# Attention inside a fused block: scores in a ring of four single PSUM banks, two of four exponentials in halves, and another order of TensorE's steps

## The chip, the cores and the metric

The kernel runs on one core of a Trainium2 chip. The metric is the device time of one execution in microseconds. A second figure is the span, from the first to the last instruction in the profile of one execution. In the text PE (or TensorE) is the matrix engine, PEld its weight load, DVE VectorE, ACT ScalarE, POOL GpSimd, and SP the engine that issues most DMAs. PSUM is the memory that TensorE writes, in eight banks; one bank holds 512 fp32 columns of 128 rows.

## The reference

One transformer block on x of 2048 x 512: pre-norm attention with 32 heads of width 16, then a gated MLP with a spatial mixing matrix.

```python
def _A_ref(x, wqkv, wo):
    B, S, D = x.shape
    H = 32; Dh = D // H
    qkv = (x @ wqkv).reshape(B, S, 3, H, Dh).transpose(2, 0, 3, 1, 4)
    q, k, v = qkv[0], qkv[1], qkv[2]
    scale = Dh ** -0.5
    scores = jnp.einsum("bhqd,bhkd->bhqk", q, k) * scale
    p = _softmax(scores, axis=-1)
    o = jnp.einsum("bhqk,bhkd->bhqd", p, v)
    return o.transpose(0, 2, 1, 3).reshape(B, S, D) @ wo
...
x = A_x
h = x + _A_ref(_layernorm(x, axis=-1), A_wqkv, A_wo)
h2 = h + _B_ref(_layernorm(h, axis=-1), B_w_in, B_w_sp, B_b_sp, B_w_out)
```

Only the attention is touched by the change. The gated MLP, `_B_ref`, is computed after it.

## The kernel before

**Stages.** First the projections to q, k and v (until about 162 us), then the attention loop (until about 1333 us), then the MLP. While the loop runs, GpSimd prepares the MLP's matrices from a list of chores that is handed out by the turn of the loop.

**Units of the attention.** Four heads form a group (`hg`, 8 of them), 512 queries a block (`qb`, 4), 128 keys a block (`kb`, 16). A unit is (hg, qb, kb); there are 512. One turn of the loop does two units, kb and kb1 = kb + 1, so there are 256 turns. The order in which each engine gets its instructions is the order in which the loop writes them (`manual_schedule`, L541); no scheduler moves them.

**Scores and exponentials.** `score` (L776) makes, for one pair p of two of the four heads, two matmuls (t = 0 and 1) of 128 keys by 512 queries, each into one bank of a tile `s` of two banks; t = 0 uses rows 0 to 49 of the matrix engine's array, t = 1 rows 64 to 113, so that two such matmuls can run side by side. One ScalarE instruction (L787) takes the exponential of all 128 x 1024 into an SBUF tile `pt`. The tiles `s` come from a pool of two (`ps_s`, L772). A unit has two such pairs, a turn four.

**Weighing.** `weigh` (L790) multiplies the values with the four exponentials of a unit, four fp32 matmuls side by side in columns of the array, and adds up over the 16 key blocks in the bank `pv`. In a turn it is called for the second unit of the turn before and for the first unit of this one. After the last key block `gather` (L798) copies `pv` out.

**Maxima.** The softmax needs each query's maximum before its scores are exponentiated. For a later block `max_pair` (L204) computes the scores of 128 queries a second time, the other way round (queries in the rows), in eight steps a turn, each a matmul of 48 rows into one of three banks `m0` to `m2`: four steps for t = 1 (`one(1, e)`) and two for t = 0 (`one(0, 2)`, `one(0, 3)`, here named `last`), each read by a VectorE maximum (L227); and for the remaining two quarters of t = 0 sums and differences of keys: `minus`, whose bank ScalarE reads with an Abs into `ab` (L232), and `plus`, whose bank VectorE reads together with `ab` (L236). Every eighth turn the maxima of 1024 rows are collected (L242 to L248) and turned by `max_rows` (L254), a VectorE transpose and eight DMAs.

The bank of each step is given by hand, as the argument of `step`: 2, 0, 1, 2, 0, 1, 2, 1. Eleven of the 256 sets of maxima (`LEAD`) are made ahead of the loop, between the projections (`ahead`, L531). So the last 11 turns have no maxima; their three banks then go to a pool `later`, and every third score tile is taken from there.

**A turn's order on TensorE** (L1043 to L1066): scores (kb, 0) and (kb, 1), two steps, `weigh` of the unit before, two steps (`minus` and `one(1, 1)`), scores (kb1, 0), a step, scores (kb1, 1), two steps (`one(1, 3)`, `plus`), `weigh` of kb, the step `last`. ScalarE's order: two exponentials, Abs, two exponentials.

Of the kernel before, what the change touches and what calls it, by code (L numbers as in the profile page):

```python
# [8 lines left out]
F32 = mybir.dt.float32  # L9
# [18 lines left out]
NB = S // P  # L28
HB = NB // 2
NQ = S // 512  # L30
# [4 lines left out]
KM = 50  # L35
PB = 6
FIRST = 2
RG = 64
# [20 lines left out]
def block_kernel(ctx: ExitStack, tc: tile.TileContext, x, wqkv, wo, w_in, w_sp4, b_sp, w_out, out):  # L59
# [7 lines left out]
    nc = tc.nc  # L67
# [131 lines left out]
    def bank(i):  # L199
        if i in more:  # L200
            return more[i]()
        return ps_m.tile([P, 512], F32, name=f"m{i}")

    def max_pair(m):  # L204

        g, i = divmod(m, 8)  # L210
        hg, qb = divmod(g, NQ)
        q, k, w = qst[g], kst[hg % 2], uvs[hg % 2]
        if i == 0:
            mx[g] = sm.tile([P, 16, 4], F32, name="mx")
            nc.gpsimd.memset(mx[g][:, :8, 3:], LOW)
        c, p = slice(i % 4 * P, i % 4 * P + P), i // 4
        at = lambda t, e: mx[g][:, t * 8 + i, e:e + 1]

        def scores(t, keys, b):
            r = slice(RG * t, RG * t + KS)  # L220
            acc = bank(b)
            nc.tensor.matmul(acc, q[r, p, c], keys[r, p], start=True, stop=True)  # L222
            return acc

        def one(t, e, b):
            acc = scores(t, k[:, :, 512 * e:512 * e + 512], b)
            nc.vector.reduce_max(at(t, e if t else e - 1), acc, axis=AX.X)  # L227

        def minus(b):
            acc = scores(0, w[:, :, 512:], b)  # L230
            ab[0] = sm.tile([P, 512], F32, name="ab")
            nc.scalar.activation(ab[0], acc, AF.Abs)  # L232

        def plus(b):
            acc = scores(0, w[:, :, :512], b)
            nc.vector.tensor_tensor_reduce(ab[0], acc, ab[0], 0.5, LOW, ALU.add, ALU.max, at(0, 0))  # L236

        def last(b):
            one(0, 3, b)
            if i == 7:  # L240
                nm = sm.tile([P, 2, 8], F32, name="nm")
                nc.vector.tensor_reduce(nm.rearrange("p t i -> p (t i)"), mx.pop(g), axis=AX.X,  # L242
                                        op=ALU.max, negate=True)
                parts = sm.tile([P, 2, 2, 8], F16, name="mparts")
                nc.gpsimd.tensor_scalar(nm, nm, 1.0 / ONE, 1.0, op0=ALU.mult, op1=ALU.mult)  # L245
                nc.gpsimd.tensor_copy(parts[:, :, 0], nm)
                nc.gpsimd.tensor_sub(parts[:, :, 1], nm, parts[:, :, 0])
                turned[0] = (g, parts)  # L248

        ab = {}  # L250
        four = [lambda b, e=e: one(1, e, b) for e in range(4)]
        return [four[0], lambda b: one(0, 2, b), minus, four[1], four[2], four[3], plus, last]

    def max_rows():  # L254

# [12 lines left out]
    with ExitStack() as pre:  # L268
        p2 = pre.enter_context(tc.tile_pool(name="pre_2", bufs=2))
        pc = pre.enter_context(tc.tile_pool(name="pre_c", bufs=1))  # L270
        pt = pre.enter_context(tc.tile_pool(name="pre_pt", bufs=2, space=PSUM))
# [257 lines left out]
        todo, done = [], [0]  # L529

        def ahead(k):  # L531
            for _ in range(k):
                m = done[0] // 8
                if not todo and m < LEAD:
                    steps = max_pair(m)
                    todo.extend(steps[i] for i in (0, 1, 3, 2, 4, 6, 5, 7))
                if todo:
                    todo.pop(0)(done[0] % 5)
                    done[0] += 1
# [67 lines left out]
        for g in range(3):  # L607
            a, b = 4 * g, 4 * g + 4
# [54 lines left out]
        for j in range(24):  # L663
            b, n, i = 1 + j // 8, j // 2 % 4, 1 - j % 2
# [21 lines left out]
            if j == 20:  # L686
                scales_ = [nc.scalar.alloc_register(f"scale{b}") for b in range(DB)]
# [78 lines left out]
    with ExitStack() as at:  # L766
# [2 lines left out]
        uvs.append(kpool1.tile([KS, 2, 1024], F16, name="uvs1"))  # L769
        fixed(kst[1])  # L770
        pp = at.enter_context(tc.tile_pool(name="pp", bufs=6))
        ps_s = at.enter_context(tc.tile_pool(name="ps_s", bufs=2, space=PSUM))  # L772
        ps_v = at.enter_context(tc.tile_pool(name="ps_v", bufs=1, space=PSUM))
        pv = {}

        def score(hg, qb, kb, p):  # L776

            q, k = qst[hg * NQ + qb], kst[hg % 2]
            turn[0] += len(later)
            pool = later[0] if turn[0] % 3 == 2 else ps_s  # L780
            s = pool.tile([P, 2, 512], F32, name="s")
            for t in range(2):
                r = slice(RG * t, RG * t + KM)
                nc.tensor.matmul(s[:, t, :], k[r, p, kb * P:(kb + 1) * P], q[r, p, :],  # L784
                                 start=True, stop=True)
            t = pp.tile([P, 2, 512], F32, name="pt")
            nc.scalar.activation(t, s, AF.Exp, scale=scales_[hg // 2])  # L787
            return t

        def weigh(hg, qb, kb, pts):  # L790
            if kb == 0:
                pv[0] = ps_v.tile([P, 512], F32, name="pv")
            for j in range(4):
                c = (4 * kb + j) * VW
                nc.tensor.matmul(pv[0][32 * j:32 * j + 32, :], vst[hg % 2][:, c:c + 32],  # L795
                                 pts[j % 2][:, j // 2, :], start=kb == 0, stop=kb == NB - 1)

        def gather(hg, qb, pool=sm):  # L798

# [39 lines left out]
        pool = nc.gpsimd  # L839
# [179 lines left out]
        prev, turn, later, asked = None, [0], [], []  # L1019
        for n in range(0, len(units), 2):  # L1020
            (hg, qb, kb), (_, _, kb1) = units[n:n + 2]
            if m % 8 < 7 and n < 480:
                work(4.1 if m % 8 < 6 else 2.0)
            if n == 480:
                work(None)
            if hg + 1 < HG and n % 64 < 24 and n % 4 == 0:
                load_k(hg + 1, [n % 64 // 4])
            if hg + 1 < HG and n % 64 < 12 and n % 4 == 2:
                load_uv(hg + 1, [n % 64 // 4])
            if hg + 1 < HG and n % 64 == 30:  # L1030
                copy_v = load_v(hg + 1)
# [10 lines left out]
            step = lambda b: steps and steps.pop(0)(b)  # L1042
            pts = [score(hg, qb, kb, 0), score(hg, qb, kb, 1)]  # L1043
            step(2)
            step(0)
            if prev is None:

                pv[0] = ps_v.tile([P, 512], F32, name="pv")
                for j in range(4):
                    nc.tensor.matmul(pv[0][32 * j:32 * j + 32, :], vst[0][:, :32],  # L1050
                                     vst[0][:, :512], start=True, stop=True)
            else:
                weigh(*prev)
            step(1)
            if kb == 0 and n:
                gather(*units[n - 1][:2])
            step(2)
            pts1 = [score(hg, qb, kb1, 0)]
            step(0)
            pts1.append(score(hg, qb, kb1, 1))  # L1060
            step(1)
            step(2)
            weigh(hg, qb, kb, pts)
            if turned:
                max_rows()
            step(1)  # L1066
            prev = (hg, qb, kb1, pts1)
            if kb == 6 and n > NB:
                invert()
            if n in (486, 490, 506):  # L1070
                asked.append(load_o(h_rows[min((n - 486) // 4, 2)]))
            if n in (492, 496, 508):
                asked.pop(0)()
            if n in (494, 502):
                split_o(h_rows[(n - 494) // 8])
            if n in (500, 504):
                sb = h_rows[(n - 500) // 4]
                make_h(sb, later[0].tile([P, 512], F32, name="h"))
# [26 lines left out]
    with ExitStack() as mid:  # L1105
# [3 lines left out]
        pt = mid.enter_context(tc.tile_pool(name="mid_pt", bufs=2, space=PSUM))  # L1109
# [278 lines left out]
```

## Time and profile before

| | |
|---|---|
| Median of three runs | 1776.86 us (1776.65 to 1778.52) |
| The profiled execution | 1777.92 us |
| Its span | 1775.8 us |
| Granted clock of TensorE, mean | 0.999 |
| First exponential, last maximum in the loop, start of the MLP | 162.1, 1284.8, 1333.4 us |

How to read the profile's lines. A group's line names the source line, the engine, the operation, the tile written, the tile read, the shapes and the count; behind the first bar stand the busy time in us and the mean of one instruction in ns, behind the second the idle time of the engine just before these instructions and what ended most of it. A line of the timeline has the start in us, the time from the first start to the last end of a merged run of equal instructions, and in brackets the idle time before it with its releaser. A line of a window has its bounds, its length, the busy time and count of PE, PEld, DVE, ACT and POOL, then the granted clock, the share of the DMA engines and GB/s. Ends of matmuls are modelled. Two instructions of one engine can overlap in the record, because the next begins before the last has written its end; the distance of two starts is the pace.

### The profile page before, as it was taken

How to read it: one execution, taken by the hardware profiler on the slowest of the kernel's cores; microseconds unless marked ns; L12 is line 12 of the kernel's file. 1: busy time of each engine (PE TensorE's matmuls, PEld its weight loads, DVE VectorE, ACT ScalarE, POOL GpSimd, SP SyncE). 2: the span in 40 equal slices, each digit the busy share in tenths (PEclk: the TensorE clock that was granted, in tenths of full speed). 3: DMA queues.
4: the chain of work that ended last, by engine and by line, in shares of the span. 5: the costliest groups of instructions: out<-in, count | busy, mean ns of one | idle time of the engine just before them, and what ended most of it. 6: DMA issues, size and time to landing. Idle time of an engine off the chain costs nothing.

```text
span 1775.8 us, 33083 instructions
## 1 busy us (share of the span) xinstructions
PE 1735.6 (98%) x11621; PEld 659.6 (37%) x11621; DVE 1409.4 (79%) x2896; ACT 1270.4 (72%) x1614; POOL 826.1 (47%) x1088
## 2 busy tenths in 40 slices
PE   9999999999999999999999999999998999999999
PEld 4433222222222222222222222222225666777776
DVE  7688999999999999999999999999926876111112
ACT  4335999999999999999999999999984555001000
POOL 1322677765762167776677757700003766010010
PEclk9999999999999999999999999999999999999999
DMA  5534332342220134435345434300033563753450
GB/s 178 158 102 147 79 83 83 79 90 69 70 66 21 56 115 126 139 115 138 92 115 135 132 100 130 98 19 9 13 71 109 139 176 112 269 196 129 148 187 24
DMA packets 183806, 191.47 MB, mean 108 GB/s; under 512 B 66344, under 2 KB 135016, under 8 KB 183640
## 3 DMA queue, kind: packets, MB, share of 16 engines
q1 hardware_dynamic: 181336, 183.72, 35.5%
q10 hardware_dynamic: 2304, 5.64, 0.8%
q8 instruction: 91, 1.49, 0.4%
q14 instruction: 75, 0.61, 0.1%
HBM read 124.40 MB, written 64.29 MB: 106 GB/s over the span
## 4 chain that ended last, share of the span: by engine, by line
PE 61%; ACT 17%; issue 9%; DVE 6%; DMA 2%; POOL 2%; SPq 1%; ACTq 0%; DVEq 0%; POOLq 0%
PE pv L795 17%; PE m L222 13%; ACT pt L787 11%; PE s L784 6%; ACT ab L232 5%; PE acc L106 4%; PE acc L108 4%; PE acc L107 4%; PE g L106 4%; PE g L108 4%; PE g L107 4%; DVE mx L227 1%; DMA rc<-r_scr 1%; DVE rs_t L123 1%; DVE rs_u L125 1%
## 5 line engine op out<-in xcount | busy, mean ns | idle before, releaser
L787 ACT ACTIVATE pt<-s 128x1024 f32<-128x1024 f32 x1024 | 995.8, 1037 | 75.4 <-PE s L784 71.8
L227 DVE TENSOR_REDUCE mx<-m 128x1 f32<-128x512 f32 x1511 | 963.7, 684 | 27.8 <-PE m L222 10.4
L795 PE MATMUL pv<-pt,vst 128*32 128x512 f32 x4096 | 551.9, 605 | 0.8 <-ACT og L802 0.8
L222 PE MATMUL m<-kst,qst 48*128 48x512 f16 x1511 | 479.3, 379 | 18.8
L784 PE MATMUL s<-qst,kst 50*128 50x512 f16 x2048 | 420.4, 379 | 2.3 <-DVE mx L227 0.6
L222 PEld LDWEIGHTS <-qst 48*128 48x128 f16 x2048 | 147.1, 94 | 539.5 <-issue 504.7
L784 PEld LDWEIGHTS <-kst 50*128 50x128 f16 x2048 | 141.5, 94 | 152.9 <-issue 75.3
L245 POOL TENSOR_SCALAR nm<-nm 128x16 f32<-128x16 f32 x32 | 6.6, 206 | 399.3 <-DVE nm L242 378.2
L222 PE MATMUL m<-uvs,qst 48*128 48x512 f16 x503 | 191.8, 381 | 0.0
L236 DVE CUSTOM_DVE_ANT_0 ab<-m,ab 128x512 f32<-128x512 f32 x252 | 171.7, 681 | 0.4 <-PE m L222 0.4
L232 ACT ACTIVATE ab<-m 128x512 f32<-128x512 f32 x251 | 151.1, 602 | 18.9 <-PE m L222 18.8
L795 PEld LDWEIGHTS pv<-pt,vst 128*32 128x32 f32 x4096 | 82.9, 108 | 183.3 <-issue 167.2
L1257 ACT ACTIVATE pT<-tp 128x384 fp32r<-128x384 f32 x32 | 14.0, 488 | 142.0 <-PE tp L1249 142.0
L1335 POOL TENSOR_TENSOR pr<-pr,z 128x344 f32<-128x344 f32 x8 | 7.3, 912 | 193.4 <-DVE pr L1334 193.4
L964 POOL TENSOR_TENSOR op<-raw,op 128x512 f16<-128x512 f32 x80 | 92.7, 1159 | 5.8
L871 POOL TENSOR_TENSOR raw<-raw 128x512 f32<-128x512 f32 (+1 forms) x84 | 83.3, 991 | 6.3
L876 POOL TENSOR_TENSOR acc_sp<-acc_sp,raw 128x512 f32<-128x512 f32 x63 | 80.3, 1275 | 4.5
L1279 DVE TENSOR_TENSOR y<-acc,h 128x512 f32<-128x512 f32 x16 | 11.1, 692 | 85.8 <-PE acc L1275 84.4
L106 PE MATMUL acc<-wi,hT 128*128 128x344 f16 x256 | 79.1, 309 | 0.0
L107 PE MATMUL acc<-wi,hT 128*128 128x344 f16 x256 | 79.1, 309 | 0.0
L108 PE MATMUL acc<-wi,hT 128*128 128x344 f16 x256 | 79.1, 309 | 0.0
L724 POOL TENSOR_TENSOR o<-o,rc 128x512 f32<-128x512 f32 x16 | 20.3, 1270 | 99.1 <-DMA rc<-r_scr 74.5
(233 smaller groups left out, 2300.4 us busy)
## 6 DMA issues: line engine op xcount, KB each, us to landing
raw<-in_w_sp SPq DMA_DIRECT2D x128, 256.0 KB
s_scr<-op SPq DMA_DIRECT2D x64, 256.0 KB
op<-s_scr SPq DMA_DIRECT2D x32, 512.0 KB
a_scr<-op SPq DMA_DIRECT2D x48, 256.0 KB
op<-a_scr SPq DMA_DIRECT2D x24, 512.0 KB
qst<-q_scr SPq DMA_DIRECT2D x192, 32.0 KB
kst<-k_scr SPq DMA_DIRECT2D x48, 128.0 KB
raw<-in_w_in SPq DMA_DIRECT2D x32, 172.0 KB
```

The costliest lines, as they stand in the source:

```text
L106: nc.tensor.matmul(ps, lh, rh, start=first, stop=False, **kw)
L107: nc.tensor.matmul(ps, lh, rl, start=False, stop=False, **kw)
L108: nc.tensor.matmul(ps, ll, rh, start=False, stop=last, **kw)
L222: nc.tensor.matmul(acc, q[r, p, c], keys[r, p], start=True, stop=True)
L227: nc.vector.reduce_max(at(t, e if t else e - 1), acc, axis=AX.X)
L232: nc.scalar.activation(ab[0], acc, AF.Abs)
L236: nc.vector.tensor_tensor_reduce(ab[0], acc, ab[0], 0.5, LOW, ALU.add, ALU.max, at(0, 0))
L784: nc.tensor.matmul(s[:, t, :], k[r, p, kb * P:(kb + 1) * P], q[r, p, :], start=True, stop=True)
L787: nc.scalar.activation(t, s, AF.Exp, scale=scales_[hg // 2])
L795: nc.tensor.matmul(pv[0][32 * j:32 * j + 32, :], vst[hg % 2][:, c:c + 32], pts[j % 2][:, j // 2, :], start=kb == 0, stop=kb == NB - 1)
L871: pool.tensor_mul(got[0] if n else acc, got[0], got[0])
L964: chores.append((lambda: pool.tensor_sub(t[0][:, 1], of(), t[0][:, 0]), TT))
```

## The change

- The four score banks become one tile `s4` of four banks, taken once ahead of the loop from a pool of one. `score` makes one matmul (one t) into one bank; a turn of two banks is chosen by a counter. In the last 11 turns a third tile `s2` from `later` joins.
- `exps` takes the exponential of two banks or, for the first pair of kb and the second pair of kb1 in turns that have maxima, of one bank at a time: two instructions of 128 x 512 in place of one of 128 x 1024.
- TensorE's order in a turn is new: step, three scores, two steps, the fourth score, `weigh` of the unit before, two steps, two scores, a step, two scores, two steps, `weigh` of kb.
- The steps' order is new (`minus` becomes the fifth, `plus` the last, `last` goes into the list `two`), and their banks go round: the count of steps modulo three. Ahead of the loop the order is changed accordingly.

```diff
-        def last(b):
-            one(0, 3, b)
             if i == 7:
...
         four = [lambda b, e=e: one(1, e, b) for e in range(4)]
-        return [four[0], lambda b: one(0, 2, b), minus, four[1], four[2], four[3], plus, last]
+        two = [lambda b, e=e: one(0, e, b) for e in (2, 3)]
+        return [four[0], four[1], two[0], four[2], minus, two[1], four[3], plus]
...
-                    todo.extend(steps[i] for i in (0, 1, 3, 2, 4, 6, 5, 7))
+                    todo.extend(steps[i] for i in (0, 2, 1, 5, 3, 4, 6, 7))
...
-        ps_s = at.enter_context(tc.tile_pool(name="ps_s", bufs=2, space=PSUM))
+        ps_s = at.enter_context(tc.tile_pool(name="ps_s", bufs=1, space=PSUM))
         ps_v = at.enter_context(tc.tile_pool(name="ps_v", bufs=1, space=PSUM))
+        s4 = ps_s.tile([P, 4, 512], F32, name="s")
...
-        def score(hg, qb, kb, p):
...
-            s = pool.tile([P, 2, 512], F32, name="s")
-            for t in range(2):
-                r = slice(RG * t, RG * t + KM)
-                nc.tensor.matmul(s[:, t, :], k[r, p, kb * P:(kb + 1) * P], q[r, p, :],
-                                 start=True, stop=True)
-            t = pp.tile([P, 2, 512], F32, name="pt")
-            nc.scalar.activation(t, s, AF.Exp, scale=scales_[hg // 2])
-            return t
+        def score(hg, qb, kb, p, t):
+
+            if not t:
+                turn[0] += 1
+                where = turn[0] % (2 + len(later))
+                s = later[0].tile([P, 2, 512], F32, name="s2") if where == 2 else s4[:, 2 * where:2 * where + 2]
+                pts[p, kb] = (s, pp.tile([P, 2, 512], F32, name="pt"))
+            r = slice(RG * t, RG * t + KM)
+            nc.tensor.matmul(pts[p, kb][0][:, t, :], kst[hg % 2][r, p, kb * P:(kb + 1) * P],
+                             qst[hg * NQ + qb][r, p, :], start=True, stop=True)
+
+        def exps(hg, kb, p, t=slice(0, 2)):
+            s, w = pts[p, kb]
+            nc.scalar.activation(w[:, t, :], s[:, t, :], AF.Exp, scale=scales_[hg // 2])
...
-            pts = [score(hg, qb, kb, 0), score(hg, qb, kb, 1)]
-            step(2)
-            step(0)
+            def step():
+                if steps:
+                    steps.pop(0)(count[0] % 3)
+                    count[0] += 1
+
+            halves = bool(steps)
+
+            def both(k, p, t):
+                score(hg, qb, k, p, t)
+                if halves and (k, p) in ((kb, 0), (kb1, 1)):
+                    exps(hg, k, p, t)
+                elif t:
+                    exps(hg, k, p)
+
+            step()
+            both(kb, 0, 0)
+            both(kb, 0, 1)
+            both(kb, 1, 0)
+            step()
+            step()
+            both(kb, 1, 1)
...
                 weigh(*prev)
-            step(1)
             if kb == 0 and n:
                 gather(*units[n - 1][:2])
-            step(2)
-            pts1 = [score(hg, qb, kb1, 0)]
-            step(0)
-            pts1.append(score(hg, qb, kb1, 1))
-            step(1)
-            step(2)
-            weigh(hg, qb, kb, pts)
+            step()
+            step()
+            both(kb1, 0, 0)
+            both(kb1, 0, 1)
+            step()
             if turned:
                 max_rows()
-            step(1)
-            prev = (hg, qb, kb1, pts1)
+            both(kb1, 1, 0)
+            both(kb1, 1, 1)
+            step()
+            step()
+            weigh(hg, qb, kb)
+            prev = (hg, qb, kb1)
```

More of the change, by code (lines that the diff above doesn't have):

```diff
@@ L771, in block_kernel, with weigh @@
         pp = at.enter_context(tc.tile_pool(name="pp", bufs=6))
-        ps_s = at.enter_context(tc.tile_pool(name="ps_s", bufs=2, space=PSUM))
+        ps_s = at.enter_context(tc.tile_pool(name="ps_s", bufs=1, space=PSUM))
         ps_v = at.enter_context(tc.tile_pool(name="ps_v", bufs=1, space=PSUM))
+        s4 = ps_s.tile([P, 4, 512], F32, name="s")
         pv = {}
-        def score(hg, qb, kb, p):
-            q, k = qst[hg * NQ + qb], kst[hg % 2]
-            turn[0] += len(later)
-            pool = later[0] if turn[0] % 3 == 2 else ps_s
-            s = pool.tile([P, 2, 512], F32, name="s")
-            for t in range(2):
-                r = slice(RG * t, RG * t + KM)
-                nc.tensor.matmul(s[:, t, :], k[r, p, kb * P:(kb + 1) * P], q[r, p, :],
-                                 start=True, stop=True)
-            t = pp.tile([P, 2, 512], F32, name="pt")
-            nc.scalar.activation(t, s, AF.Exp, scale=scales_[hg // 2])
-            return t
-        def weigh(hg, qb, kb, pts):
+        def score(hg, qb, kb, p, t):
[10 more added lines that the diff above has]
+            nc.scalar.activation(w[:, t, :], s[:, t, :], AF.Exp, scale=scales_[hg // 2])
+        def weigh(hg, qb, kb):
             if kb == 0:
@@ L795, in weigh @@
                 nc.tensor.matmul(pv[0][32 * j:32 * j + 32, :], vst[hg % 2][:, c:c + 32],
-                                 pts[j % 2][:, j // 2, :], start=kb == 0, stop=kb == NB - 1)
+                                 pts[j % 2, kb][1][:, j // 2, :], start=kb == 0, stop=kb == NB - 1)
+            for p in range(2):
+                del pts[p, kb]
         def gather(hg, qb, pool=sm):
@@ L1018, in block_kernel @@
         units = [(hg, qb, kb) for hg in range(HG) for qb in range(NQ) for kb in range(NB)]
-        prev, turn, later, asked = None, [0], [], []
+        prev, turn, count, later, asked, pts = None, [1], [0], [], [], {}
         for n in range(0, len(units), 2):
@@ L1041, in block_kernel @@
                     tc.tile_pool(name="ps_l", bufs=1, space=PSUM, side="right")))
-            step = lambda b: steps and steps.pop(0)(b)
-            pts = [score(hg, qb, kb, 0), score(hg, qb, kb, 1)]
-            step(2)
-            step(0)
+            def step():
[16 more added lines that the diff above has]
+            both(kb, 1, 1)
             if prev is None:
```

## The prediction

> **What bounds the kernel now.** I read the page first (busy shares, chain, groups), then the stages as windows, then the chain and the timeline of one turn of the attention loop. Page:
>
> ```profile
> PE 1735.6 (98%) x11621; PEld 659.6 (37%) x11621; DVE 1409.4 (79%) x2896; ACT 1270.4 (72%) x1614; POOL 826.1 (47%) x1088
> ...
> L787 ACT ACTIVATE pt<-s 128x1024 f32<-128x1024 f32 x1024 | 995.8, 1037 | 75.4 <-PE s L784 71.8
> L227 DVE TENSOR_REDUCE mx<-m 128x1 f32<-128x512 f32 x1511 | 963.7, 684 | 27.8 <-PE m L222 10.4
> L795 PE MATMUL pv<-pt,vst 128*32 128x512 f32 x4096 | 551.9, 605 | 0.8 <-ACT og L802 0.8
> L222 PE MATMUL m<-kst,qst 48*128 48x512 f16 x1511 | 479.3, 379 | 18.8
> L784 PE MATMUL s<-qst,kst 50*128 50x512 f16 x2048 | 420.4, 379 | 2.3 <-DVE mx L227 0.6
> L784 PEld LDWEIGHTS <-kst 50*128 50x128 f16 x2048 | 141.5, 94 | 152.9 <-issue 75.3
> L236 DVE CUSTOM_DVE_ANT_0 ab<-m,ab 128x512 f32<-128x512 f32 x252 | 171.7, 681 | 0.4 <-PE m L222 0.4
> L232 ACT ACTIVATE ab<-m 128x512 f32<-128x512 f32 x251 | 151.1, 602 | 18.9 <-PE m L222 18.8
> ```
>
> Three engines are nearly full, and the share alone doesn't say which sets the pace. The stages, as windows:
>
> ```profile
> 162.10:1284.80 1122.70, 1101.65 (x7840) 288.55 (x7837) 1098.19 (x2093) 1054.11 (x1255) 656.18 (x860) 1.00 0.32 88
> 1284.80:1333.40 48.60, 46.98 (x296) 10.88 (x294) 10.96 (x31) 42.23 (x47) 4.45 (x6) 1.00 0.33 76
> 1333.40:1776.00 442.60, 428.98 (x2715) 290.35 (x2712) 176.73 (x502) 113.83 (x208) 126.66 (x159) 1.00 0.45 149
> ```
>
> The first window (span, then PE, PEld, DVE, ACT and POOL busy, clock, DMA) is the attention loop while it also makes maxima: 256 - 11 = 245 turns in 1122.7 us, **4.58 us a turn**. Then 11 turns without maxima (48.6 us), then all that the change does not touch. One turn in the chain of waits:
>
> ```profile
> 742.09 0.50 ACT ab L232
> 742.63 0.43 PE m L222 x2
> 743.06 1.00 PE pv L795 x8
> 744.06 0.32 PE m L222
> ...
> 744.91 0.72 issue
> 745.63 1.02 ACT pt L787
> 746.64 0.50 ACT ab L232
> ```
>
> From one Abs to the next (742.09 to 746.64, 4.55 us): Abs frees a maxima bank, TensorE, which goes strictly in order, gets past the step that waited for that bank, does a `weigh` (1.00), and only then the scores for which ScalarE stands idle. So a turn is a loop of waits between TensorE and ScalarE, not a full engine. Price of each hop (timeline of one turn):
>
> ```profile
> 734.85 0.68 PE L784 MATMUL s<-qst,kst 50*128 50x512 f16 x3
> 735.14 0.09 PEld L784 LDWEIGHTS <-kst 50*128 50x128 f16 x1 [0.19 <-issue]
> 735.36 0.40 PE L222 MATMUL m<-kst,qst 48*128 48x512 f16 x2
> 735.64 1.02 ACT L787 ACTIVATE pt<-s 128x1024 f32<-128x1024 f32 x1 [0.54 <-PE s L784]
> 735.68 0.63 PE L795 MATMUL pv<-pt,vst 128*32 128x512 f32 x3
> ```
> ```profile
> 733.13 1.96 ACT L787 ACTIVATE pt<-s 128x1024 f32<-128x1024 f32 x2
> 735.64 1.94 ACT L787 ACTIVATE pt<-s 128x1024 f32<-128x1024 f32 x2 [0.54 <-PE s L784]
> 737.46 0.60 ACT L232 ACTIVATE ab<-m 128x512 f32<-128x512 f32 x1
> 737.94 1.04 ACT L787 ACTIVATE pt<-s 128x1024 f32<-128x1024 f32 x1
> ```
> ```profile
> 736.68 0.39 PE L222 MATMUL m<-uvs,qst 48*128 48x512 f16 x1
> ...
> 738.12 0.37 PE L222 MATMUL m<-kst,qst 48*128 48x512 f16 x1
> ```
> ```profile
> 147.64 0.38 PE L222 MATMUL m<-uvs,qst 48*128 48x512 f16 x1
> ...
> 148.09 0.60 ACT L232 ACTIVATE ab<-m 128x512 f32<-128x512 f32 x1 [2.36 <-PE m L222]
> ```
>
> - An exponential ends at 733.13 + 1.96 = 735.09, and the score that waited for its bank starts with its weights at 735.14: **0.05** from ScalarE to TensorE. The same at 738.12, behind the Abs that ended at 738.06.
> - A lone matmul started at 147.64 is read at 148.09: **0.45** from TensorE to ScalarE. For a pair of scores (735.15) it is **0.49** (735.64).
> - A matmul on rows just used starts **0.21** after the one ahead of it (735.15 to 735.36).
> - `weigh` starts 0.32 after the last small matmul (735.36 to 735.68) and lets the next one through 1.00 later (736.68): **1.32**.
> - Abs to exponential: **0.48** (737.46 to 737.94).
>
> **The change part by part.** *What it says*: a score no longer waits for a two-bank tile but for one bank, and the first and fourth exponential of a turn become halves, so that each starts behind one matmul. *What the changed program does* is told by its list of instructions with the counts they wait for. All four banks are one tile, `s4`, taken once ahead of the loop. Of a steady turn (h: a half, F: a whole exponential; kb, kb1 the two key blocks; the newest ScalarE instruction that must have ended is on the right):
>
> ```
> S(kb,0,0)    waits for h(kb1,1,1) of the turn before
> S(kb,0,1)    waits for h(kb,0,0)     (other bank)
> S(kb,1,0)    waits for h(kb,0,1)     (other bank)
> S(kb,1,1)    no further wait
> S(kb1,0,0)   waits for F(kb,1)       (other bank)
> S(kb1,0,1)   no further wait
> S(kb1,1,0)   waits for F(kb1,0)      (other bank)
> S(kb1,1,1)   waits for h(kb1,1,0)    (other bank)
> ```
>
> Each score waits for the last exponential that read **any** of the four banks. Before, each waited for the exponential two tiles back. So the ring is a ring of one: score, exponential, score, exponential. That is the whole forecast; everything else is small beside it.
>
> One turn, with TensorE's new order (M0 to M7 the steps; M4 is `minus`, whose reader is Abs): M0, S, S, S, M1, M2, S, weigh, M3, M4, S, S, M5, S, S, M6, M7, weigh. A half is taken at the 0.60 of the Abs of the same 128x512 (L232); bounds: above half of a 1024 (0.52), below a whole one (1.04). From the turn's first score at 0:
>
> 1. h(kb,0,0): 0.45 + 0.60 + 0.05 = 1.10, S(kb,0,1) starts.
> 2. h(kb,0,1): 1.10 more, S(kb,1,0) at 2.20.
> 3. M2 uses the same rows: +0.21; S(kb,1,1) beside it, at 2.41.
> 4. `weigh` of the unit before: +1.32, M3 and M4 at 3.73. F(kb,1) runs meanwhile (2.41 + 0.45 to 3.90) and is covered.
> 5. M4 to Abs +0.49 (a pair), Abs to F(kb1,0) +0.48: 4.70. The scores for it start at 3.95 and would be ready at 4.44, so Abs, queued ahead of it on ScalarE, decides.
> 6. F(kb1,0) 1.04 + 0.05: S(kb1,1,0) at 5.79.
> 7. h(kb1,1,0): +1.10, S(kb1,1,1) at 6.89.
> 8. M6, M7 behind it +0.21, `weigh` +1.32: 8.42, the next turn's M0 and S. Its own wait, for h(kb1,1,1), ended at 6.89 + 1.10 = 7.99 and is covered.
>
> Sum: 3 x 1.10 + 2 x 0.21 + 2 x 1.32 + 0.49 + 0.48 + 1.09 = **8.42 us** against 4.58: +3.84 x 245 = **+940 us**.
>
> *Costs at nothing.* Two more ScalarE instructions a turn (4 x 0.60 for 2 x 1.04, +0.33 us of recorded time) lie in ScalarE's new idle time, apart from the halves counted above. VectorE has 6 x 0.68 + 0.68 = 4.8 us of work in 8.4, so the rotation of the maxima's banks frees each long before its M. GpSimd's queue is handed out by turns, not by time, and has more room; SP's few DMAs a turn likewise, and the maxima's transpose with its eight DMAs, which stands some instructions earlier, has a whole group of turns until its rows are read. The order of steps ahead of the loop changes for 11 maxima under projections: nothing, within 3 us.
>
> *The 11 turns without maxima.* No halves; a third tile joins the rotation, but two of three uses are still in `s4`. By the same hops six exponentials (three units, with three `weigh`) take about 7.25 us, so a turn of four 4.83 against 48.6/11 = 4.42: +5 us.
>
> *The clock.* TensorE will have gaps of some 1.2 us (from M5 at 4.2 to S(kb1,1,0) at 5.8) and be busy about 60% of a turn. Rows that bear on it:
>
> ```profile
> 1333.40:1336.80 3.40, 1.25 (x9) 0.51 (x6) 2.26 (x3) 1.48 (x3) 1.27 (x1) 1.00 0.20 59
> ```
> ```profile
> 1369.25 0.61 PE L106 MATMUL acc<-wo,o 128*128 128x512 f16 x1 [2.58 <-ACT o L729]
> 1369.65 0.63 PE L107 MATMUL acc<-wo,o 128*128 128x512 f16 x1
> ```
>
> In a window with 1.25 of 3.40 us busy the clock stayed 1.00; only behind 2.58 us of nothing does a matmul take 0.61 and the next start 0.40 later. So I count the full clock. The Trainium skill, "TensorE: Matmul & The Clock Gate" (section "A second HAM failure mode: psum-queue depth-cycling"), speaks against it: a kernel that cycles through PSUM banks can idle briefly so often that the clock swings between half and full. No stretch of this trace shows that; it is a rival below.
>
> **Forecast.** The profiled execution took 1777.92 us, 2.1 more than its span; 1775.8 + 940 + 5 + 2.1 = 2723. It stood 1.1 above the median, so **2722 us**.
>
> **Rivals.**
>
> - *The waits are per bank after all* (the change does what it says). Then VectorE's maxima decide:
>
> ```profile
> 699.37 3.07 DVE L227 TENSOR_REDUCE mx<-m 128x1 f32<-128x512 f32 x5
> ...
> 702.36 0.68 DVE L236 CUSTOM_DVE_ANT_0 ab<-m,ab 128x512 f32<-128x512 f32 x1
> ```
>
>   Reductions start (3.07 - 0.68)/4 = 0.60 apart. Three of them (1.80), `plus` and its release (0.74), M2 to S 0.21, `weigh` 1.32, M3 to its reduction 0.45: 4.52 for a turn, at most 0.21 less if that score pairs with M2; with the 0.03 by which the mean now exceeds the chain, 4.55 or 4.34: 1777 - 7 = 1770, at best 1777 - 59 = 1718. Faster, if the wait counts don't mean what I read. 3%.
> - *`weigh` and Abs leave the loop*: scores and exponentials alone, 4 x 1.10 + 2 x (0.49 + 1.09) = 7.56: 1777 + 245 x 2.98 + 5 = 2512. It needs TensorE to run a `weigh` while a score ahead of it waits; in the chain above it never does. Up to 2640 for mixtures. 8%.
> - *Dearer hops*: weights loaded only behind each wait (94 ns by the page, five times a turn) and 0.49 at each of three halves: 8.42 + 0.47 + 0.12 = 9.01, 2867. The 0.05 measured at a waiting score speaks against it. 6%.
> - *Half clock*: 0.21 becomes 0.40, `weigh` doubles its 1.00, each of four hops to ScalarE takes 0.23 more (0.61 for 0.38): 8.42 + 0.38 + 2.00 + 0.92 = 11.7, about 3530; part of the time, near 3100. 5%.
>
> **How the numbers follow.** The forecast has 78%, for turns of 8.2 to 8.75 us: 2670 to 2805. The range takes in the near ends of the second and third rival: 2640 to 2850. A measurement here can tell some 0.2% from no change. The first rival splits into faster 2% and the same 1%; slower 97%.
>
> **What would show it.** Right: 980 exponentials of 128x512 near 0.60 and 534 of 128x1024; the stage with maxima near 2063 us, a turn 8.4; ScalarE and VectorE each near 60% busy there; ScalarE idle for scores and TensorE for exponentials, in turn; clock 1.00; the last stage still 443 us. Wrong: two scores of different banks running ahead of one exponential (waits per bank), a `weigh` of more than 1.0 us (clock), or a score that starts well over 0.05 behind the exponential that it waits for.

## The result and the profile after

| | before | changed |
|---|---|---|
| Median | 1777.53 us (4 runs) | 3400.99 us (4 runs, 3387.42 to 3410.3) |
| Ratio of the medians | | 1.9128, 95% interval 1.9089 to 1.9166 |
| Profiled execution, span | 1777.92, 1775.8 us | 3387.42, 3385.4 us |
| Mean granted clock of TensorE | 0.999 | 0.663 |
| Mean distance of two Abs (one turn) | 4.58 us | 11.11 us |

The change nearly doubles the time. The forecast was 2722 us with a range up to 2850: the direction was right, the size was far off.

The page of the changed kernel, with the lines that answer to those shown of before (busy time and share of each engine; the clock in forty slices, in tenths; the groups):

```profile
PE 2628.2 (78%) x11621; PEld 701.8 (21%) x11621; DVE 1477.6 (44%) x2896; ACT 1432.4 (42%) x2104; POOL 821.5 (24%) x1088
...
PEclk9955565555555565566556566555655566999999
...
L788 ACT ACTIVATE pt<-s 128x512 f32<-128x512 f32 (+1 forms) x1514 | 1128.6, 747 | 1199.8 <-PE s L783 1062.4
L783 PE MATMUL s<-qst,kst 50*128 50x512 f16 x2048 | 935.5, 558 | 740.6 <-ACT pt L788 740.6
L795 PE MATMUL pv<-pt,vst 128*32 128x512 f32 x4096 | 897.5, 964 | 0.0
L222 PE MATMUL m<-kst,qst 48*128 48x512 f16 x1510 | 810.9, 577 | 0.0
```

Two things are to be seen, and they are different. First, the idle times at the right ends: ScalarE was idle 71.8 us for scores before, now 1062.4; TensorE's scores waited 2.3 us, now 740.6, all of it for exponentials. The two engines work in turn. Second, the same matmuls take longer: a score 558 ns on the mean for 379, a `weigh` matmul 964 for 605. The counts of matmuls are equal (11621). The clock line fits this: about half speed from the third slice to the end of the attention loop.

The stages, as windows (span, PE, PEld, DVE, ACT, POOL, clock, DMA share, GB/s): the turns with maxima, those without, and the rest:

```profile
162.10:2892.00 2729.90, 2001.02 (x7890) 332.39 (x7889) 1165.86 (x2094) 1223.02 (x1754) 654.44 (x864) 0.58 0.13 37
2892.00:2950.00 58.00, 44.95 (x278) 12.33 (x277) 13.70 (x34) 37.54 (x42) 3.81 (x3) 0.94 0.20 50
2950.00:3386.00 436.00, 423.62 (x2682) 287.18 (x2680) 174.04 (x497) 111.78 (x204) 124.57 (x158) 0.99 0.45 150
```

The whole loss lies in the first window, where the clock is 0.58. From the first exponential to the last Abs of the loop there were 1120.3 us before (162.1 to 1282.4) and 2714.2 now (161.7 to 2875.9): +1594. From there to the end of the span 493.4 became 509.5: +16. Together that is the 1610 us by which the spans differ.

The list of waits in the first window (who waits for whom: us in all, times, longest) shows the ring:

```profile
ACT pt L788 <- PE s L783: 1049.7, 985, 2.3
PE s L783 <- ACT pt L788: 729.4, 983, 1.4
```

983 waits of a score for an exponential are four a turn in 245 turns. And the chain of one turn (start, length, what):

```profile
1000.51 0.58 PE s L783
1001.09 0.43 PE m L222 x2
1001.54 1.86 PE pv L795 x7
1003.41 0.58 PE m L222 x2
1004.01 0.42 ACT ab L232
...
1004.51 1.03 ACT pt L788
...
1005.58 0.59 PE s L783
1006.19 0.61 ACT pt L788
...
1006.84 0.58 PE s L783
1007.42 0.43 PE m L222 x2
1007.85 1.86 PE pv L795 x8
1009.71 0.54 PE m L222
...
1010.32 0.60 ACT pt L788
...
1010.97 0.60 PE s L783
1011.59 0.61 ACT pt L788
...
1012.24 0.58 PE s L783
```

From 1000.51 to 1012.24 one turn takes 11.73 us. The order of its pieces is that of the eight hops of the prediction: score, half, score, half, score, `weigh`, Abs, whole exponential, score, half, score, `weigh`. But every piece on TensorE has its half-clock length: `weigh` 1.86 for 1.00, a pair of maxima 0.43 for 0.22, a score that lets ScalarE go after 0.6.

Where the clock is full for a moment, the hops have the predicted size. The timeline of TensorE, first a score behind a wait at half clock, then two at full clock:

```profile
1006.84 0.58 PE L783 MATMUL s<-qst,kst 50*128 50x512 f16 x1 [0.69 <-ACT pt L788]
...
1017.30 0.37 PE L783 MATMUL s<-qst,kst 50*128 50x512 f16 x1 [1.20 <-ACT pt L788]
1018.36 0.37 PE L783 MATMUL s<-qst,kst 50*128 50x512 f16 x1 [0.68 <-ACT pt L788]
```

At full clock the second starts 1.06 us behind the first (predicted 1.10); at half clock the same step takes 1.26 (1005.58 to 1006.84, in the chain above).

### The profile page after: what moved, and what is told of

It reads as the page before. It is cut to its first block, busy times and chain, and to the rows that moved or that the text cites. A ratio compares the mean times of both kernels' runs of the same rounds, so it can differ in the third digit from the quotient of the medians.

```text
span 3385.4 us, 33103 instructions
## 1 busy us (share of the span) xinstructions
PE 2628.2 (78%) x11621; PEld 701.8 (21%) x11621; DVE 1477.6 (44%) x2896; ACT 1432.4 (42%) x2104; POOL 821.5 (24%) x1088
## 4 chain that ended last, share of the span: by engine, by line
PE 68%; ACT 25%; issue 3%; DVE 3%; DMA 0%; POOL 0%; SPq 0%; ACTq 0%; DVEq 0%; POOLq 0%
PE pv L795 25%; ACT pt L788 21%; PE s L783 16%; PE m L222 13%; ACT ab L232 3%; PE acc L106 2%; PE acc L108 2%; PE acc L107 2%; PE g L106 2%; PE g L108 2%; PE g L107 2%; DVE rs_t L123 0%; DVE og L803 0%; ACT og L804 0%; DVE rs_u L125 0%
## 5 line engine op out<-in xcount | busy, mean ns | idle before, releaser
L227 DVE TENSOR_REDUCE mx<-m 128x1 f32<-128x512 f32 x1510 | 1014.7, 689 | 1524.5 <-PE m L222 1340.0
L788 ACT ACTIVATE pt<-s 128x512 f32<-128x512 f32 (+1 forms) x1514 | 1128.6, 747 | 1199.8 <-PE s L783 1062.4
L783 PE MATMUL s<-qst,kst 50*128 50x512 f16 x2048 | 935.5, 558 | 740.6 <-ACT pt L788 740.6
L795 PE MATMUL pv<-pt,vst 128*32 128x512 f32 x4096 | 897.5, 964 | 0.0
L222 PE MATMUL m<-kst,qst 48*128 48x512 f16 x1510 | 810.9, 577 | 0.0
L783 PEld LDWEIGHTS <-kst 50*128 50x128 f16 x2048 | 173.9, 110 | 716.5 <-issue 711.3
L222 PE MATMUL m<-uvs,qst 48*128 48x512 f16 x504 | 272.0, 541 | 0.0
L963 POOL CAST op<-raw 128x512 f16<-128x512 f32 x80 | 48.8, 610 | 284.4 <-DMA s_scr<-op 141.7
L855 POOL TENSOR_SCALAR raw<-raw,figs 128x512 f32<-128x512 f32 (+1 forms) x84 | 55.5, 665 | 34.4 <-DMA raw<-in_w_in 20.1
L870 POOL TENSOR_SCALAR raw<-raw 128x512 f32<-128x512 f32 (+1 forms) x88 | 52.1, 592 | 40.4 <-DMA raw<-in_w_in 20.8
```

The costliest lines, as they stand in the source:

```text
L783: nc.tensor.matmul(pts[p, kb][0][:, t, :], kst[hg % 2][r, p, kb * P:(kb + 1) * P], qst[hg * NQ + qb][r, p, :], start=True, stop=True)
L788: nc.scalar.activation(w[:, t, :], s[:, t, :], AF.Exp, scale=scales_[hg // 2])
```

## The experiments

Two theories. **Ring and clock**: the forecast's mechanism is right, each score waits for the newest exponential of any bank of the one tile `s4`, and the rest of the loss is the clock. The rival: the loss comes from **the order or the halves** (more instructions on ScalarE, the steps' new places), and the clock follows. Each diff is against the changed kernel unless it says otherwise. The kernel before took 1777 to 1779 us (medians) beside these runs.

### own_tiles: score banks as tiles of their own

```diff
-        s4 = ps_s.tile([P, 4, 512], F32, name="s")
+        s1 = [ps_s.tile([P, 512], F32, name=f"s{b}") for b in range(2)]
+        s2 = ps_s.tile([P, 2, 512], F32, name="s")
```

The p = 0 pairs use the two single tiles and halves, the p = 1 pairs the double tile and whole exponentials; so the second pair that is halved is (kb1, 0) here, for (kb1, 1) in the change, and the last 11 turns have no third tile. TensorE's order and the steps stay as in the change.

> The changed kernel with its four banks as three tiles (two of one bank, one of two); the first pair of both units in halves, the second whole. Theory (each score of the change waits for the newest exponential of any of the four banks, and the clock falls because of the gaps): with waits per tile the loop is score to M2, weigh, Abs, two halves, a whole exponential: 0.21 + 1.32 + 0.49 + 0.48 + 0.95 + 1.09 = 4.54 us a turn, clock 1.00, about 1770 us in all. Rival (the halves or the new order of steps are to blame, not the shared tile): the time stays far over 2000 us.

Measured: 1781.54 us, 9 runs; ratio 1.0021 (1.0011 to 1.0031), clock 0.999, a turn 4.54 (median). The new order and four halves a turn are still there, and 1619 us are gone. These tiles, too, are taken once ahead of the loop, as `s4` is. So neither the order nor the halves as such are the cause, nor that a tile is taken once; which banks share a tile is.

### order_only: the order without the ring and without halves

```diff
-        s4 = ps_s.tile([P, 4, 512], F32, name="s")
-                s = later[0].tile([P, 2, 512], F32, name="s2") if where == 2 else s4[:, 2 * where:2 * where + 2]
+                s = later[0].tile([P, 2, 512], F32, name="s2") if where == 2 else ps_s.tile([P, 2, 512], F32, name="s")
-                if halves and (k, p) in ((kb, 0), (kb1, 1)):
-                    exps(hg, k, p, t)
-                elif t:
+                if t:
                     exps(hg, k, p)
```

> The change's order of TensorE's steps and its rotation of the maxima's banks alone: score tiles of two banks from a pool of two, four whole exponentials, as before. Theory: the order costs nothing; score to M2, weigh, Abs, two exponentials 0.21 + 1.32 + 0.49 + 0.48 + 0.90 + 1.09 = 4.49 a turn against 4.58, 1755 to 1775 us, clock 1.00. Rival (the order puts weigh where it blocks the scores): 1850 us or more.

Measured: 1777.2 us, 10 runs; ratio 0.9994 (0.9985 to 1.0004). Here `ps_s` is a pool of two again. The order and the rotation of the maxima's banks cost nothing and bring nothing. They did change what bounds a turn. Its chain:

```profile
704.61 0.37 PE m L222 x2
704.98 0.69 DVE mx L227
...
705.71 0.39 PE m L222 x2
706.10 0.99 PE pv L794 x8
```

A maximum on VectorE now stands where Abs stood in the chain before: one wait took the other's place.

### ring_only: the ring's tile without the order and without halves

Against the kernel before (cut to the lines that matter; the pool holds one tile, and the counter of tiles starts one later):

```diff
+        s4 = ps_s.tile([P, 4, 512], F32, name="s")
...
-            pool = later[0] if turn[0] % 3 == 2 else ps_s
-            s = pool.tile([P, 2, 512], F32, name="s")
+            s = later[0].tile([P, 2, 512], F32, name="s2") if where == 2 else s4[:, 2 * where:2 * where + 2]
```

> The kernel before with only its score tiles replaced by one tile of four banks; whole exponentials, the old order and the old banks of the maxima. Theory: each pair of scores waits for the whole exponential ahead of it. At the full clock: two exponentials' hops 1.58 + 1.58 with a weigh beside the second, Abs ahead of the third (3.6 to 4.1), 1.04 + 0.05 to the fourth score, 0.21 + 0.32 + 1.00 + 0.20 to the next turn: 6.9 us a turn, 2350 us if the clock stays, about 2850 if it falls as in the change. Rival (the ring alone is harmless, the halves make the chain): 1780 us.

Measured: 2413.88 us (one execution), clock 0.963, a turn 6.85 at full clock. One turn in the chain of this kernel:

```profile
700.88 1.03 ACT pt L788
...
701.95 0.39 PE s L785 x2
...
702.56 1.00 PE pv L796 x8
703.56 0.32 PE m L222
703.88 0.24 PE s L785
...
704.21 1.03 ACT pt L788
...
705.28 0.39 PE s L785 x2
...
707.74 1.03 ACT pt L788
```

From 700.88 to 707.74, 6.86 us. Whole exponentials, the old order, and nothing new but the one tile: +636 us, of which the longer turn at full clock is 245 x 2.27 = 556. The scores use the same four banks in the same rotation as before; only which exponential a score waits for has changed. In the chain each pair of scores starts behind the exponential just ahead of it (701.91 to 701.95, 705.24 to 705.28), in place of the one two tiles back.

### no_halves and halves_own_pool: the other two corners

`no_halves` keeps ring and order and takes four whole exponentials; `halves_own_pool` keeps order and halves and takes the score tiles from a pool of two.

```diff
 no_halves
-                if halves and (k, p) in ((kb, 0), (kb1, 1)):
-                    exps(hg, k, p, t)
-                elif t:
+                if t:
 halves_own_pool
-                s = later[0].tile([P, 2, 512], F32, name="s2") if where == 2 else s4[:, 2 * where:2 * where + 2]
+                s = later[0].tile([P, 2, 512], F32, name="s2") if where == 2 else ps_s.tile([P, 2, 512], F32, name="s")
```

> The changed kernel with its one tile of four banks and its order, but four whole exponentials a turn. Theory: 1.58 to the second pair, 0.21, weigh 1.32, Abs 0.49 and 0.48 to the third exponential, 1.09 to the fourth pair, 0.21 and weigh 1.32 to the next turn: 6.7 us, the emptiest window near 51%, so the clock stays above 0.9: 2300 to 2420 us. Rival (the halves cost nothing, the tile all): the change's 8.4 us or more a turn, 2720 to 3400 us.

> The change's order and its two halved exponentials, but score tiles of two banks from a pool of two, as before; the second score of a halved pair still waits for the first half, since both are in one tile. Theory: scores of the other tile run ahead, but TensorE's order holds them behind the waiting one: first half 1.10, third and fourth score 0.43, weigh 1.32, Abs and its exponential 0.97, the halves behind it 1.55, the last steps and weigh 1.53: 6.9 us a turn, 2350 us at the full clock, up to 2700 if it falls. Rival (the halves are harmless without the four-bank tile): 1780 us.

Measured, one execution each: `no_halves` 2446.46 us, clock 0.949, a turn 6.88 (median); just above the range expected. `halves_own_pool` 3043.09 us, clock 0.648: a turn of 6.94 where the clock was full, as expected (6.9), and 10.15 (median) where it was half; the time is far above the 2700 expected at most, since the clock fell much more than was allowed for. A half in a tile of two banks makes a wait even with tiles of their own for the pairs: the second score of a pair goes to the other bank of the same tile and waits for the half that reads the first. In its chain, at half clock, the half ends at 1011.53 and the score starts at 1011.57:

```profile
1010.92 0.61 ACT pt L787
...
1011.57 0.61 PE s L782 x2
```

The two kernels have the same turn at full clock (6.88 and 6.94) and differ by 597 us through the clock. With `order_only` and `own_tiles` these runs close the rival: the halves cost nothing where each halved bank has its own tile, and make waits where it hasn't.

### fill_four: the clock held up

Four of the eight maxima's matmuls are done 4, 4, 6 and 4 times (the same result again) and put in TensorE's gaps; three steps move for this.

```diff
+    times_ = {(1, 0): 4, (1, 1): 4, (0, 3): 6, (1, 3): 4}
...
-            nc.tensor.matmul(acc, q[r, p, c], keys[r, p], start=True, stop=True)
+            for _ in range(n):
+                nc.tensor.matmul(acc, q[r, p, c], keys[r, p], start=True, stop=True)
```

> The changed kernel with the same waits, but four of a turn's maxima matmuls done 4, 4, 6 and 4 times into their own bank, and moved to where TensorE would wait for an exponential (14 matmuls more a turn, the output the same). Theory (two causes: the chain of waits, and the clock that falls because TensorE stands idle too often): the clock returns to 1.00 and the turn becomes 3 x 1.10 + 0.21 + 2 x 1.32 + 0.49 + 0.48 + 1.09 = 8.2 us, about 2670 us in all, faster than the change in spite of more work. Rival (the slow matmuls come from the chain itself, not from idleness): the clock stays near 0.6, the matmuls that are added no longer fit the gaps, and the time is 3400 us or more.

Measured: 2653.37 us (one execution), clock 0.996, a turn 8.05 (median). A stretch of the loop:

```profile
162.10:1200.00 1037.90, 1016.18 (x5874) 311.47 (x5873) 610.26 (x1096) 633.40 (x910) 373.82 (x506) 1.00 0.17 49
```

With 14 more matmuls a turn the kernel is 750 us faster than the change, and the clock stays at 1.00. The turn that is left, 8.05, is the ring's price at full clock in this order of the steps, for which 8.2 was expected (the change's own order: 8.42). VectorE and ScalarE are busy 59% and 61% of this window, as forecast for the change.

### fill_one and fill_first: less filling

`fill_one` does one step, `one(0, 3)`, six times and leaves the order alone; `fill_first` does the first two steps four times each and moves them behind the first and the second score.

```diff
 fill_one
+    times_ = {(0, 3): 6}
 fill_first
+    times_ = {(1, 0): 4, (1, 1): 4}
```

> The changed kernel with one matmul of a turn's maxima, the fourth-quarter step ahead of the second scores of kb1, done six times into its own bank (1.07 us more of TensorE's time a turn, all in the gap from 4.2 to 5.8). Theory (the clock falls behind a window of 3.41 us, free-running, in which TensorE streams for less than about 47%, and comes back behind one of about 88%): the emptiest stretch, 35%, is filled, the next one, at the turn's start, has 46% and is met rarely: clock over 0.92, 8.4 to 8.9 us a turn, 2720 to 2850 us. Rival (the mean share decides): the same as the run that fills the start.

> The changed kernel with the first two steps of a turn's maxima done four times each, between the first three scores (1.28 us more a turn; they move behind the first and second score). Theory (a low window decides): the mean share of a turn is lifted as much as in the run that fills the one later gap, but the stretch from 3.7 to 7.1 keeps its 35%, so the clock falls nearly every turn, and comes back behind the filled start: clock 0.65 to 0.85, 9 to 10.8 us a turn, 2870 to 3300 us. Rival (the mean share, or the number of gaps, decides): 2850 us or less, clock over 0.92.

Measured, one execution each: `fill_one` 3587.29 us, clock 0.650, a turn 11.94 on the mean; `fill_first` 3659.42 us, clock 0.641, a turn 12.25. Both missed, `fill_one` by 740 us, `fill_first` by 360. The rule behind the expectation, that the clock falls when TensorE streams less than some 47% of the time, fell with it: TensorE streamed more than in the change and kept no more clock. The added matmuls, now at half clock, only made the turn longer.

### fill_rows: the same filling with full rows

The next theory: the clock goes not by the time in which matmuls stream but by that time weighted by the share of the array's 128 rows in use. The maxima's matmuls use 48, the scores 50. `fill_rows` is `fill_one` with the five added matmuls over 128 rows of zeros in place of 48 rows of keys.

```diff
+    rows128 = const.tile([P, 512], BF, name="rows128")
...
+            for _ in range(n):
+                nc.tensor.matmul(acc, rows128[:, :P], rows128, start=True, stop=True)
             nc.tensor.matmul(acc, q[r, p, c], keys[r, p], start=True, stop=True)
```

> As the run that fills the one later gap, but the five extra matmuls there read 128 rows of zeros in place of 48 rows of queries (same five times 512 columns, same place, overwritten by the real one behind them). Theory (the clock follows the share of a 3.41 us window weighted by the rows of the array in use; it falls under 0.40 and comes back over 0.78): the emptiest stretch rises from 0.19 to 0.51 at the full clock and only the turn's start, 0.37, is under the bound, for some 0.4 us of the 8.4 a window can start in: clock over 0.88, 8.4 to 9.2 us a turn, 2720 to 2920 us. Rival (rows don't count, only the time in which TensorE streams): as with 48 rows, clock 0.65, 3590 us.

Measured: 2885.52 us (one execution), clock 0.928, a turn 9.07 on the mean, within what was expected. The same stretch of `fill_one`, then of `fill_rows`:

```profile
300.00:1200.00 900.00, 740.18 (x2794) 146.98 (x2790) 360.15 (x644) 373.83 (x537) 225.45 (x300) 0.57 0.11 28
```
```profile
300.00:1200.00 900.00, 692.88 (x3663) 151.45 (x3663) 470.41 (x852) 490.47 (x705) 272.41 (x373) 0.90 0.15 40
```

As many added matmuls (1225), of nearly the same recorded length at full clock (376 and 379 ns): the clock is 0.57 in one and 0.90 in the other. One turn at full clock in the chain of `fill_rows`, from a score to the same score of the next turn, takes 8.30 us:

```profile
721.35 0.37 PE s L788
...
727.23 1.19 PE m L226 x5
...
729.65 0.37 PE s L788
```

The five added matmuls stand in this chain where Abs and the whole exponential stand in the prediction's hops. The timelines of ScalarE and TensorE show that they lengthen nothing: the whole exponential ends at 727.52 + 1.02 = 728.54, and the score that waits for it starts 0.05 behind.

```profile
727.52 1.02 ACT L793 ACTIVATE pt<-s 128x1024 f32<-128x1024 f32 x1
...
728.59 0.37 PE L788 MATMUL s<-qst,kst 50*128 50x512 f16 x1
```

### own_tiles_all: the change as it reads

Four tiles of one bank, all exponentials in halves (eight a turn for the change's four), the change's order, no third tile in the last 11 turns. This is the ring of four single banks that the title names.

```diff
-        s4 = ps_s.tile([P, 4, 512], F32, name="s")
+        s4 = [ps_s.tile([P, 512], F32, name=f"s{b}") for b in range(4)]
...
-                if halves and (k, p) in ((kb, 0), (kb1, 1)):
-                    exps(hg, k, p, t)
-                elif t:
-                    exps(hg, k, p)
+                exps(hg, k, p, t)
```

> A ring of four single banks that is one: four tiles of one bank, every exponential in halves (eight of 128x512 a turn, in the turns without maxima too), the change's order. Theory: no wait but for its own bank; ScalarE has 9 x 0.48 = 4.3 us a turn and the loop through weigh and the maxima's reductions stays at about 4.53: 1765 to 1790 us, clock 1.00. Rival (single banks let TensorE run ahead and shorten the turn): 4.35 us a turn, 1725 us.

Measured: 1764.24 us, 4 runs; ratio 0.9922 (0.9902 to 0.9943): 0.8% below the kernel before, just under the 1765 to 1790 expected. The turns with maxima, and the chain:

```profile
162.10:1270.00 1107.90, 1076.03 (x7833) 279.67 (x7833) 1081.55 (x2091) 1102.06 (x2234) 656.21 (x860) 1.00 0.33 89
```
```profile
720.32 0.37 PE m L222 x2
720.68 0.69 DVE mx L227
...
721.42 0.39 PE m L222 x2
721.81 0.99 PE pv L794 x8
...
724.77 0.37 PE m L222 x2
```

A turn takes 4.45 here (720.32 to 724.77) and 4.52 on the mean. The exponentials left the chain: the list of waits, which has those over 0.15 us, has no wait of an exponential for a score from 300 to 1200 us. VectorE's maximum stands in the chain, at the place where the prediction's first rival put it. But ScalarE is all but full as well, busy 1102.06 of 1107.90 us: its halves follow each other 0.477 us apart at the least, and with Abs (0.52 behind a half, 0.49 ahead of the next) a turn's nine instructions need about 7 x 0.477 + 0.52 + 0.49 = 4.35 of the 4.46 us (median) that a turn takes. The chain does not tell which of the two would set the pace if the other were relieved. The last Abs starts at 1268.0 for 1282.4 before: these 14.4 us are the whole gain.

## Why the prediction was wrong, point by point

- **The ring of one: right.** The waits as listed (983, four a turn) and the chain show it. `ring_only` shows it alone (+2.27 us a turn), `own_tiles_all` its absence. The rival *the waits are per bank after all* did not come true of the change; the kernel where they are, `own_tiles_all`, took 1764, inside that rival's 1718 to 1770, and has in its chain the wait that it names; it takes four more halves a turn than the rival had, and ScalarE is nearly full there too.
- **The eight hops, 8.42 us a turn: right at full clock within 5%.** `fill_rows`, in the change's order, has 8.30 for a turn at full clock; three hops of a half at 1.06 for 1.10 make up the 0.12. `fill_four`, whose order saves one 0.21, measured 8.05 for its 8.2. A half took 597 ns in the changed kernel's loop (predicted 600):

```profile
L788 ACT ACTIVATE pt<-s 128x512 f32<-128x512 f32 x980 | 585.1, 597 | 890.5 <-PE s L783 753.5 <-PE m L222 136.9
```

- **Costs at nothing: right.** Order and banks: `order_only`, 0.9994. More ScalarE instructions: `own_tiles` and `own_tiles_all`.
- **"So I count the full clock": this step failed.** The clock in the loop was 0.58. Of the 1594 us, the hops explain 245 x (8.30 to 8.42, less 4.58) = 910 to 940 us, and the clock the other 650 to 680. The price that the *Half clock* rival gave, 11.7 us a turn, is what the chain shows (11.73); mixed with full-clock turns of 8.30 at a clock of 0.58, which is 84% of the time at half, it gives 1 / (0.16/8.30 + 0.84/11.73) = 11.0 us, and 11.11 were measured. So that rival had the mechanism and its price at half clock; its figure for a mixture, near 3100, was low, and its chance, 5%, far too small. The Trainium skill's warning in "TensorE: Matmul & The Clock Gate" (section "A second HAM failure mode: psum-queue depth-cycling"), which the prediction cited and set aside, is what this trace shows: the clock fell 130 times in the loop.
- **Why the step failed.** It took two rows for evidence that were none. The window of 3.40 us with 1.25 us busy was cut where it suited the reader; the clock has its own windows of 3.413 us (below), and the stretch shown fell into two of them, which by the weighting below have shares of 0.38 and 0.63. And the "busy about 60% of a turn" counted a matmul of 48 rows like one of 128. Weighted by rows, the turn's share at full clock is (16 x 0.21 x 0.39 + 2 x 1.00) / 8.3 = 0.40, just where the clock falls; before, the same 3.3 us in a turn of 4.58 give 0.72. The two could have been compared beforehand.
- **The 11 turns without maxima: +5 forecast.** The stretch from the last Abs to the end grew by 16 us, some of it at a clock of 0.94. Small, and not separated further.
- **ScalarE and VectorE near 60% busy:** 45% and 43% in the change, through the longer turn; 61% and 59% in `fill_four`.

## What to carry to other kernels

Ask of each tile what a wait on it covers: banks cut from one tile were waited for as one, and four tiles in place of one tile of four banks, with every exponential in halves, turned a factor of 1.91 into a gain of 0.8% here. Before you count on the full clock in a loop that gets new gaps, add up TensorE's streaming time over windows of 3.4 us with each matmul weighted by the rows that it uses (the weight that fits these kernels best), and compare it with a stretch whose clock the trace shows. Where a mechanism is priced at two clocks, as here with 8.42 and 11.7, the range has to reach to the second price unless a row excludes it.

## What the runs showed of the hardware

**The clock goes by free-running windows and by rows.** The trace of each run lists the changes of the granted clock: only 1.0 and 0.5 occur in these loops, and the changes lie whole multiples of 3.413 us apart. In the changed kernel 127 of 129 spells at full clock last exactly one window. I added up, for each such window in the loop, the streaming time of every matmul (its record less 0.165 us: a score is recorded with 0.379 and lets the next one start after 0.21), scores and maxima weighted 0.39 (48 to 50 of 128 rows), `weigh` 1 (its four matmuls side by side a quarter each), the zeros of `fill_rows` 1, as a share of the window. Of the windows after which the clock fell, the largest share, and of those after which it came back, the smallest:

```
kernel            falls  largest share   returns  smallest share   median unweighted share of falling windows
changed            130      0.39           130        0.78               0.50
ring_only           19      0.39            19        0.76               0.71
no_halves           26      0.38            26        0.78               0.66
halves_own_pool     27      0.39            27        0.77               0.58
fill_first         109      0.35           109        0.79               0.45
fill_one           109      0.40           109        0.79               0.74
fill_rows          120      0.39           120        0.84               0.61
fill_four            3      0.37             3        0.78               0.93
before, own_tiles_all  0      -              0         -                  -
```

With this weight the clock fell only below about 0.40 and came back only above about 0.76, in the eight kernels in which it fell. Without it (last column) there is no such bound: `fill_one` falls at a median of 0.74, while the full-clock windows of `no_halves` that stay have a median of 0.75. The two bounds far apart explain why a spell at half clock lasts: the change's turn at half clock has about (16 x 0.40 x 0.39 + 2 x 1.86) / 11.73 = 0.53. The separation is not perfect: 134 windows with 0.36 to 0.40 kept the full clock, 94 of them in `fill_rows`, and some 200 windows at half clock with 0.77 to 0.80 did not bring it back. Nor is the weight exact: 0.35 to 0.43 parts falling windows from kept ones about equally well (51 to 60 of the 3947 windows at full clock in twelve kernels are on the wrong side of the best bound), 0.5 less well (90), 1 badly (267).

A rule of the Trainium skill, "TensorE: Matmul & The Clock Gate" (section "Why this matters for your kernels"), asks for no idle gap of TensorE above some 3 us. It is not enough here: the longest wait of a score in the loop was 1.4 us, and the clock fell 130 times.

**Open.** The weight was told apart by one pair of kernels, `fill_one` and `fill_rows`, whose added matmuls differ in type (bf16 for f16) and in values (zeros) too; `weigh`, the other one with full weight, is fp32. So rows are the likeliest reason and not the only one possible. Why a fall lasts some 23 windows in `halves_own_pool` and two to three in `no_halves`, with nearly the same turn at full clock, was not settled beyond where the two `weigh` of a turn fall in a window.
